# Score tiles of 64x64, masks made on the chip, paged memory and a fixed list of finer steps in a three-part kernel

## The chip, the cores and the metric

The program runs on one core of a Trainium2 chip. A core has five engines that matter here, each with its own in-order queue: PE (matrix products), DVE and POOL (element-wise work), ACT (functions such as exp, sin and gelu, and copies) and SP (which issues the loads and stores). The metric is the device time of one execution in microseconds, the median of several. The time before is 423.65 us (three runs, 423.07 to 424.15).

## The reference

Three parts follow one another, on 2 batches of 768 tokens:

1. Attention with 8 heads of 64. Every query sees the keys less than 16 positions away, and beside them 24 summaries of blocks of 32 keys (the maximum of the keys, the mean of the values). One softmax runs over both:

```
scores_l_m = np.where(mask_l, scale * q @ k^T, -1e9)            # mask_l: |i - j| < 16
scores_s   = scale * q @ k_sum^T + log(32)
a = softmax(concat([scores_l_m, scores_s]))
out = a @ concat([v, v_sum])
```

2. A rotation and a mix over tokens, with d_model 512 (x is the attention's output, all heads side by side):

```
theta = x @ w_theta
y = w_tok_r @ (x * cos(theta)) + w_tok_i @ (x * sin(theta))
u = x + y;   x = u + relu(u @ w_ch)
```

3. A gated block: `h = gelu(x @ w_in)`, split into u and v of 512 columns; v is normalised over its columns and times g_ln; `v_s = w_sg @ v + b_sg` mixes tokens; the output is `x + (u * v_s) @ w_out`.

All of it is float32.

## The kernel before

**Products.** A float32 product is three products: each operand is split into a high part (a rounded copy, L257 to L264) and a low part (the difference, L267), and `mm3` (L269 to L274) adds hi·hi, hi·lo and lo·hi. So L272, L273 and L274 stand for all dense products, in pieces of 512 or 256 columns: theta, the token mix y, ch (u @ w_ch), iv and iu (x @ w_in), sg (w_sg) and o (w_out). A weight comes in by a DMA (L346) and is put together by ACT (L357, `t`) and DVE (L363, `r`), or comes in whole (w_sg, L375); it is copied as its high part by ACT or POOL (`h`) and gets its low part by DVE or POOL (`l`).

**Attention.** It works in 16 units: a unit is a pair of heads and half of a batch's tokens (384 queries). `S` (L485 to L499) makes the scores of both heads in two PSUM banks of 128x360: per head first a product of identity and mask (L485, 128x360), then the near scores in 64x64 tiles of PE (L492, 12 products of 64x96), then the scores against the 24 summaries in tiles of 64x128 (L499, 6 products of 128x24). Then DVE takes the maximum (`m`, L509, both heads in one step) and subtracts it (`d`, L517), ACT does exp (L523), PE transposes (`PT`, L528), ACT or DVE copies (`Pt`), PE multiplies by the values (`O`, L542), DVE divides by the sum (`n`, L552 to L556), PE transposes the result (`X`, L565) and it is copied and split (`xe`, `xh`, `xl`). The key summaries `ks` are made by DVE (L440), the value summaries `vs` by DVE (L448) or POOL (L451, L453); PE turns them (`vp`) and they are spread into the value tiles (`vm`, `vr`). Identity and masks come by one DMA of 244 KB (`cst`, L299), and DVE turns them into bf16 (L301 to L308). Eight products of a tile of zeros (`fill`, L314) open PE's work.

**Rotation.** For each of 12 theta tiles: `kk` and `kb` on ACT, `ra` (L605) and `rr` (L611) on DVE, `ab` (L626, L627), two sines on ACT (`sc`), the product with x (`zm`, L641), high and low part (`zh`, `zl`). y adds up over the 6 token tiles of a batch; it comes in two column halves for each batch, and in each step of six products it needs one z tile and the weights w_r or w_i and w_ri of its token tile. `uv` (L689) adds y to x.

**The order.** No loop sets it. Every step is declared with its engine or engines, what it follows, what memory it takes and a due time (`key`). `Order.play` (L95 to L175) then plays the whole program against a table of costs, takes at each turn the engine that can start first and the most urgent step that it can start, chooses between engines where several may do a step, and so writes down one order. The steps are emitted in that order; every engine runs its own part of it in order. A dense chain (all contraction blocks of ch, iv, iu, sg or o into one bank) is one step, 12 or 18 products long, and so waits for all its operands.

**The memory.** Fixed slots (L206, L207): 27 of 4 KB a partition, 19 of 2 KB, 4 of 6 KB, and small ones; each tile takes a whole slot of its kind, and a load can be issued only when a slot of its kind is free and some are left over (`spare`). [...]

Of the kernel before, what the change touches and what calls it, by code (L numbers as in the profile page):

```python
# [9 lines left out]
F32 = mybir.dt.float32  # L10
# [10 lines left out]
DM = 512  # L21
P = 128
# [14 lines left out]
PI_LO = 3.1415925  # L37

class Op:
# [3 lines left out]
class Order:  # L45

    LAT = {"PE": 0.16, "DVE": 0.09, "ACT": 0.09, "POOL": 0.09, "SP": 0.0}
    RATE = 3.1e-6  # L50
    TABLE = 1.29
    PATIENCE = {"PE": 0.1, "DVE": 0.1, "ACT": 0.1, "POOL": 0.1, "SP": 0.0}

    def __init__(self, slots):
        self.ops, self.by = [], {}
        self.slots, self.kind, self.uses = slots, {}, {}

    def op(self, name, eng, fn, after=(), new=(), use=(), key=None, tab=None, spare=0, size=0,
           port=(), lead=0.0, early=0.0):
        o = Op()  # L60
        o.name, o.eng, o.fn, o.key, o.tab, o.spare = name, eng, fn, key, tab, spare
        o.size, o.port, o.lead, o.early = size, port, lead, early
        o.after, o.new = set(after), list(new)
        o.use = list(use) + [b for b, _ in new]
        o.succ, o.pre, o.left = [], [], len(o.after)
        assert name not in self.by, name
        self.by[name] = o
        self.ops.append(o)
        for b, k in new:
            self.kind[b] = k  # L70
        for b in o.use:
            self.uses[b] = self.uses.get(b, 0) + 1
        return name

    def link(self):

        for o in self.ops:
            for a in o.after:
                self.by[a].succ.append(o)
        left = {o: len(o.succ) for o in self.ops}  # L80
        todo = [o for o in self.ops if not left[o]]
        while todo:
            o = todo.pop()
            d = min(o.eng.values()) + 0.1
            if o.size:
                d = 2.0 + o.size * self.RATE
            k = min((s.key for s in o.succ), default=1e6) - d - o.lead
            o.key = k if o.key is None else o.key
            for a in o.after:
                a = self.by[a]  # L90
                left[a] -= 1
                if not left[a]:
                    todo.append(a)

    def play(self):  # L95
        self.link()
        free_at = {"PE": 1.4, "DVE": 0.7, "ACT": 2.0, "POOL": 0.7, "SP": 0.7}
        slots = {k: [(0.0, s) for s in v] for k, v in self.slots.items()}
        uses, ends, self.where = dict(self.uses), {}, {}
        port = dma = 0.0  # L100
        table = "none"
        waiting = [o for o in self.ops if not o.left]
        out = []

        def able(o, e):
            t = max(free_at[e], o.early)
            for end, on in o.pre:
                t = max(t, end if on == e else end + self.LAT[on])
            return max(t, port) if e in o.port else t

        def room(o):
            t = 0.0
            kinds = [k for _, k in o.new]
            for k in set(kinds):
                c = kinds.count(k) + o.spare
                if len(slots[k]) < c:
                    return None
                t = max(t, sorted(slots[k])[c - 1][0])
            return t

        while waiting:
            found = {}
            for o in waiting:
                t = room(o)
                if t is not None:
                    for e in o.eng:
                        found.setdefault(e, []).append((max(t, able(o, e)), o))
            assert found, [o.name for o in waiting]
            picks = []
            for e, c in found.items():  # L130
                s0 = min(s for s, _ in c) + self.PATIENCE[e]

                def rank(x):
                    o = x[1]
                    turn = 4.0 if e == "ACT" and o.tab and o.tab != table else 0.0
                    return (o.key + turn, x[0])
                s, o = min((x for x in c if x[0] <= s0), key=rank)
                picks.append((s, e, o))
            s, e, o = min(picks, key=lambda x: (x[0], x[1] != "POOL"))
            if len(o.eng) > 1:  # L140

                t = room(o)
                for e2, d in o.eng.items():
                    s2 = max(t, able(o, e2))
                    if (s2 + d < s + o.eng[e] - 0.02
                            and not any(x.key < o.key and q <= s2 + d for q, x in found[e2])):
                        e, s = e2, s2
            if e == "ACT" and o.tab and o.tab != table:
                table = o.tab
                s = max(s, free_at[e]) + self.TABLE  # L150
            waiting.remove(o)
            f = free_at[e] = s + o.eng[e]
            if e in o.port:
                port = f
            if o.size:
                dma = max(dma, s + 1.1) + o.size * self.RATE
                f = dma + 0.9
            o.start, o.end, o.on = s, f, e
            for b, k in o.new:
                j = max((x for x in slots[k] if x[0] <= s + 1e-9), key=lambda x: x[0])  # L160
                slots[k].remove(j)
                self.where[b] = j[1]
            for b in o.use:
                uses[b] -= 1
                ends[b] = max(ends.get(b, 0.0), f + self.LAT[e])
                if not uses[b]:
                    slots[self.kind[b]].append((ends[b], self.where[b]))
            for q in o.succ:
                q.pre.append((f, e))
                q.left -= 1  # L170
                if not q.left:
                    waiting.append(q)
            out.append(o)
        assert len(out) == len(self.ops), [o.name for o in self.ops if o not in out][:20]
        return sorted(out, key=lambda o: o.start)  # L175
# [3 lines left out]
def kernel(  # L179
# [22 lines left out]
    EN = {"PE": nc.tensor, "DVE": nc.vector, "ACT": nc.scalar, "POOL": nc.gpsimd, "SP": nc.sync}  # L202
    PE, DVE, ACT, POOL = nc.tensor, nc.vector, nc.scalar, nc.gpsimd


    SIZE = {"W": 1024, "H": 512, "X": 3 * DM, "K": NS, "V": VC, "Z": 512, "B": 512}  # L206
    COUNT = {"W": 27, "H": 19, "X": 4, "K": 12, "V": 3, "Z": 3, "B": 8}  # L207
    order = Order({k: [f"{k}{j}" for j in range(n)] for k, n in COUNT.items()})
    op = order.op
    made = {}  # L210

    def T(name, dt=F32, fresh=False):

        if name not in made or fresh:
            k = order.kind[name]
            n = SIZE[k] * 4 // mybir.dt.size(dt)
            made[name] = (ps_ if k == "B" else cp).tile([P, n], dt, tag=order.where[name],
                                                        name=name)
        return made[name]


    cst = cp.tile([P, P + 3 * WC], F32, tag="cst", name="cst")
    ident = cst[:, :P]
    identb = cp.tile([P, P], BF16, tag="identb", name="identb")
    maskb = cp.tile([P, 2, 3, WC], BF16, tag="maskb", name="maskb")
# [4 lines left out]

    def act(n):
        return 0.20 + 0.00083 * n

    def dve(n):
        return 0.15 + 0.00105 * n

    def dve1(n):
        return 0.15 + 0.00053 * n

    def pool1(n):  # L240
        return 0.12 + 0.00100 * n

    def pool2(n):
        return 0.12 + 0.00250 * n

    PORT = ("DVE", "POOL")

    def copies(n, es, psum=False):

        d = {"ACT": act(n), "DVE": dve(n) if psum else dve1(n), "POOL": pool1(n)}  # L250
        return {e: d[e] for e in es}

    def diffs(n, es):
        d = {"DVE": dve(n), "POOL": pool2(n)}
        return {e: d[e] for e in es}

    def copy(e, dst, src):  # L257
        if e == "ACT":
            ACT.activation(dst, src, AF.Copy)  # L259
        elif e == "POOL":  # L260
# [14 lines left out]

    def sl(c, n=P):
        return slice(c * n, (c + 1) * n)

    def cut(hl, s):
        return hl[0][:, s], hl[1][:, s]  # L280


    def set_consts(e):
        POOL.memset(half_pi[:], math.pi / 2)
        POOL.memset(eps_t[:], 1e-6)
        for j in range(COUNT["Z"]):
# [712 lines left out]
```

## Time and profile before

| | |
|---|---|
| device time, median of 3 (lowest to highest) | 423.65 us (423.07 to 424.15) |
| span of the profiled execution | 417.5 us |
| what lies around the span (median less span) | 6.15 us |
| PE busy | 397.3 us, 95% |
| DVE busy | 251.6 us, 60% |
| ACT busy | 191.1 us, 46% |
| POOL busy | 111.2 us, 27% |
| loads and stores | 40.71 MB, 98 GB/s over the span |

The span is the time from the first to the last instruction of one profiled execution, and all durations of rows come from that execution. Its own device time is not listed beside it, so the median stands for it. [...] Where the text speaks of a pace, it is the distance between starts in an unbroken row of like instructions.

### The profile page before, as it was taken

The page shows a single profiled execution, that of the slowest core. Times are in us where ns is not written, and L with a number is a line of the kernel's source. Part 1 is how long each engine was busy: PE and PEld are TensorE (multiplying, and loading weights), DVE is VectorE, ACT ScalarE, POOL GpSimd, SP SyncE. Part 2 cuts the span into 40 slices and gives each one's busy share as a digit, 9 for nine tenths or more (in the row PEclk, how much of TensorE's full clock was granted, in tenths as well). Part 3 has the DMA queues.
Part 4 walks back from the last instruction along what each step waited for, and adds up shares of the span by engine and source line. Part 5 has one row for each costly group of instructions (what it writes and reads, how often), then busy time and mean ns, then how long its engine had stood idle before and what let it go on. Part 6 is the DMA issues. An engine that isn't in the chain of part 4 may idle for free.

```text
span 417.5 us, 7283 instructions
## 1 busy us (share of the span) xinstructions
PE 397.3 (95%) x2880; PEld 330.3 (79%) x2880; DVE 251.6 (60%) x459; ACT 191.1 (46%) x332; POOL 111.2 (27%) x147
## 2 busy tenths in 40 slices
PE   7999798989899599999999999999999999999996
PEld 3777576867778388888888898888888989888876
DVE  6589879888966577443564785539574231565222
ACT  2488788876865686224133621435633123421000
POOL 2374663463520523121267521101101000000000
PEclk9699999999999789999999999999999999999999
DMA  8999944341005801200227100100400000210222
GB/s 256 309 325 396 315 155 120 105 124 50 2 2 158 344 2 51 75 2 7 70 83 226 58 2 0 52 0 1 152 0 0 2 0 8 94 52 25 102 75 101
DMA packets 17233, 40.71 MB, mean 98 GB/s; under 512 B 2096, under 2 KB 7600, under 8 KB 17200
## 3 DMA queue, kind: packets, MB, share of 16 engines
q1 hardware_dynamic: 17200, 40.26, 29.6%
q8 instruction: 22, 0.36, 0.4%
q14 instruction: 11, 0.09, 0.1%
HBM read 37.11 MB, written 3.15 MB: 96 GB/s over the span
## 4 chain that ended last, share of the span: by engine, by line
PE 80%; DMA 9%; DVE 6%; issue 1%; ACT 1%; POOL 1%; SPq 0%; DVEq 0%; ACTq 0%
PE y L274 5%; PE y L273 5%; PE y L272 5%; PE sg L274 4%; PE sg L273 4%; PE sg L272 4%; PE ch L272 3%; PE ch L274 3%; PE ch L273 3%; PE iu L274 3%; PE iu L272 3%; PE iu L273 3%; PE iv L274 3%; PE iv L272 3%; PE iv L273 3%; PE ys L274 3%
## 5 line engine op out<-in xcount | busy, mean ns | idle before, releaser
L267 DVE TENSOR_TENSOR z<-f,z 128x512 fp32r<-128x512 f32 x19 | 14.4, 758 | 23.9 <-POOL z L261 20.2
L272 PE MATMUL ys<-w_ri,z 128*128 128x256 f32 x96 | 27.3, 284 | 0.5 <-POOL w_ri L261 0.5
L273 PE MATMUL ys<-w_ri,z 128*128 128x256 f32 x96 | 27.4, 285 | 0.3 <-DVE w_ri L267 0.3
L274 PE MATMUL ys<-w_ri,z 128*128 128x256 f32 x96 | 27.2, 283 | 0.0
L261 POOL TENSOR_SCALAR z<-f 128x512 fp32r<-128x512 f32 x17 | 10.9, 640 | 48.6 <-PE ys L274 27.4
L860 DVE SCALAR_TENSOR_TENSOR gf<-sg,g_sb,bsg 128x512 f32<-128x512 f32 (+1 forms) x16 | 9.9, 616 | 22.5 <-PE sg L274 22.4
L272 PEld LDWEIGHTS ys<-w_ri,z 128*128 128x128 f32 x96 | 18.4, 192 | 5.1 <-POOL w_ri L261 1.0
L272 PE MATMUL y<-w_r,z 128*128 128x512 f32 x48 | 19.9, 415 | 2.7 <-POOL z L261 1.7
L273 PEld LDWEIGHTS ys<-w_ri,z 128*128 128x128 f32 x96 | 18.3, 191 | 5.2 <-DVE w_ri L267 0.8
L272 PE MATMUL th<-w_th,xh 128*128 128x512 f32 x48 | 20.2, 420 | 2.0 <-ACT w_th L259 1.7
L274 PE MATMUL y<-w_r,z 128*128 128x512 f32 x48 | 19.7, 411 | 1.7 <-DVE z L267 1.6
L273 PE MATMUL y<-w_r,z 128*128 128x512 f32 x48 | 19.6, 409 | 0.9 <-POOL w_r L267 0.9
L273 PE MATMUL th<-w_th,xh 128*128 128x512 f32 x48 | 19.0, 395 | 1.0 <-DVE w_th L267 1.0
L509 DVE TENSOR_REDUCE m<-S 128x3 f32<-128x360 f32 x32 | 15.5, 525 | 6.9 <-PE S L499 6.7
L273 PE MATMUL y<-w_i,z 128*128 128x512 f32 x48 | 19.3, 401 | 0.3 <-DVE w_i L267 0.3
L272 PE MATMUL y<-w_i,z 128*128 128x512 f32 x48 | 19.5, 406 | 0.0
L274 PE MATMUL y<-w_i,z 128*128 128x512 f32 x48 | 19.2, 399 | 0.0
L274 PE MATMUL th<-w_th,xh 128*128 128x512 f32 x48 | 18.9, 394 | 0.0
L273 PE MATMUL sg<-w_sg,vn 128*128 128x512 f32 x48 | 18.9, 394 | 0.0
L272 PE MATMUL sg<-w_sg,vn 128*128 128x512 f32 x48 | 18.9, 394 | 0.0
L274 PE MATMUL sg<-w_sg,vn 128*128 128x512 f32 x48 | 18.9, 394 | 0.0
L542 PEld LDWEIGHTS O<-v,Pt 120*64 120x64 f32 x384 | 13.8, 145 | 6.3 <-issue 2.2
(314 smaller groups left out, 1233.5 us busy)
## 6 DMA issues: line engine op xcount, KB each, us to landing
v<-in_vW_dram SPq DMA_DIRECT2D x16, 290.2 KB, 7.9
k<-in_kT_dram SPq DMA_DIRECT2D x8, 384.0 KB, 4.5
q<-in_qT_dram SPq DMA_DIRECT2D x16, 192.0 KB, 6.2
vT<-in_vT_dram SPq DMA_DIRECT2D x8, 384.0 KB, 5.9
w_r<-in_w_rT_dram SPq DMA_DIRECT2D x6, 511.8 KB, 7.3
w_i<-in_w_iT_dram SPq DMA_DIRECT2D x6, 511.8 KB, 6.5
w_th<-in_w_theta_dram SPq DMA_DIRECT2D x4, 511.8 KB, 8.9
w_ch<-in_w_ch_dram SPq DMA_DIRECT2D x4, 511.8 KB, 8.4
```

What stands on the lines that cost most here:

```text
L261: POOL.tensor_scalar(out=dst, in0=src, scalar1=1.0, scalar2=0.0, op0=ALU.mult, op1=ALU.add)
L267: EN[e].tensor_tensor(out=lo, in0=src, in1=hi.bitcast(F32), op=ALU.subtract)
L272: PE.matmul(ps, ah, bh, start=first, stop=False, skip_group_check=True)
L273: PE.matmul(ps, ah, bl, start=False, stop=False, skip_group_check=True)
L274: PE.matmul(ps, al, bh, start=False, stop=last, skip_group_check=True)
L509: DVE.tensor_reduce(out=T(f"m{u}")[:, 3 * h:3 * h + 3], in_=s3(h), axis=AX.X, op=ALU.max)
L542: PE.matmul(ps[64 * ab:64 * ab + 64, o:o + 65], sb[:WC, t * P + 64 * ab:t * P + 64 * ab + 64], v[:WC, c:c + 65], start=True, stop=True)
L860: DVE.scalar_tensor_tensor(out=gf, in0=T(bk)[:, :n], scalar=g_sb[:, f:f + 1], in1=T("bsg")[:, o:o + n], op0=ALU.mult, op1=ALU.add)
```

## The change

- **Scores in 64x64 tiles throughout.** The mask is added by 4 products of 64x(3x96) per unit in place of 2 of 128x360, and the summaries' scores are made by 12 products of 64x24 in place of 6 of 128x24. `m` is two steps, one a head.
- **Masks made by POOL.** DVE fills identity and masks with constants, and 14 `affine_select` instructions on POOL cut them to shape; DVE makes the bf16 identity and one copied mask. The DMA of `cst` is gone, and with it L299 to L308.
- **Memory in pages.** One area of 2760 pieces of 64 bytes in pages of 192 pieces (12 KB); a tile is a piece of any size at an address. A page holds one kind at a time: F (float32) or R (the split float32r form). When a step puts the other kind into it, the page is taken anew under the same tag, so that the first writer follows all users of the page's earlier content.
- **A fixed list.** `Order` with its costs and keys is gone. `PLAN` names every step with its engine and the addresses of what it makes, and `Steps.play` emits them as they stand.
- **Finer steps.** A dense chain has one step for each contraction block (`chain`: three products), so that steps of other chains can stand between them.

Of the list two of its lines are shown; the others are of the same form.

```diff
+AREA, PAGE = 2760, 192
...
+k1.S.2712 ones.V masks.G q0_0.S.2688 q1_0.S.168 warm.V.148 fill.P.0 k0.S.100 ks1.V.0 q2_1.S.76
+identb.V S1_0.P.0.1 ks0.V.1 m1_0_1.V.2 m1_0_0.V.3 q0_1.S.52 S0_1.P.2.3 vT0.S.4 vT1.S.336 k2.S.288
...
+    def play(self, plan):
+        done = set()
+        for step in plan.split():
+            name, e, *at = step.split(".")
+            o = self.all[name]
+            assert all(a in done for a in o.after) and e in o.eng and len(at) == len(o.new), name
+            for (b, kind, n), a in zip(o.new, at):
+                self.where[b] = self.place(kind, n, int(a))
+            o.fn(e)
+            done.add(name)
...
+    def place(kind, n, a):
+        if kind in "FR":
+            j, a = divmod(a, PAGE)
+            if pages.get(j, "-")[0] != kind:
+                w = 16 * min(PAGE, AREA - j * PAGE)
+                pages[j] = kind, cp.tile([P, w], F32 if kind == "F" else F32R, tag=f"page{j}",
+                                         name=f"page{j}{kind}")
+            return pages[j][1][:, 16 * a:16 * a + n // 4]
...
+    def set_masks(e):
+        select(ident, [[-1, P]], 0, 1, 0.0)
+        select(ident, [[1, P]], 0, -1, 0.0)
+        for j, o in ((0, 0), (1, 16), (4, 32)):
+            for r in (0, 64):
+                m = maskb[r:r + 64, j]
+                select(m, [[1, WK]], 15 - o, -1, NEG)
+                select(m, [[-1, WK]], 15 + o, 1, NEG)
...
         def scores(e):
             k, q, ks = T(f"k{p}"), T(f"q{u}"), T(f"ks{p}")
-            s = [T(f"S{u}_{h}") for h in range(2)]
-            for h in range(2):
-                PE.matmul(s[h][:, :3 * WC], identb[:], maskb[:, hf].rearrange("p t c -> p (t c)"),
-                          start=True, stop=False, skip_group_check=True)
+            for ab in range(2):
+                for h in range(2):
+                    rr, m = slice(64 * h, 64 * h + 64), hf + ab
+                    PE.matmul(s3(h)[sl(ab, 64), :, :WK], identb[rr, rr], maskb[rr, m:m + 3],
+                              start=True, stop=False, skip_group_check=True)
...
             for t in range(3):
-                for h in range(2):
-                    rr = slice(64 * h, 64 * h + 64)
-                    PE.matmul(s[h][:, t * WC + WK:(t + 1) * WC], q[rr, sl(t)], ks[rr, :],
-                              start=False, stop=True, skip_group_check=True)
+                for ab in range(2):
+                    for h in range(2):
+                        rr = slice(64 * h, 64 * h + 64)
+                        PE.matmul(s3(h)[sl(ab, 64), t, WK:], q[rr, sl(2 * t + ab, 64)],
+                                  ks[rr, :], start=False, stop=True, skip_group_check=True)
...
+    def chain(bk, n, terms):
+
+        for j, (an, a, bn, b) in enumerate(terms):
+            op(f"{bk}_{j}", "P",
+               lambda e, a=a, b=b, j=j: mm3(T(bk)[:, :n], a(), b(), j == 0, j == len(terms) - 1),
+               after=[an + "l", bn + "l"] + [f"{bk}_{j - 1}"] * (j > 0),
+               use=[an, bn] + [bk] * (j > 0), new=[] if j else [(bk, "B", 1)])
+        return f"{bk}_{len(terms) - 1}"
```

What the list moves is seen in the instructions of each engine. The first place is POOL's start. Before, POOL sets its constants (half_pi, eps, zero, ones) and then makes its first copy, that of the ones into a value tile; the ISA row is the instruction that loads POOL's function library.

```order
L284 MEMSET half_pi 128x1
L285 MEMSET eps_t 128x1
L288 MEMSET zero_72 128x512
L288 MEMSET zero_74 128x512
L288 MEMSET zero_76 128x512
L292 MEMSET ones_78 128x1
L292 MEMSET ones_80 128x1
L292 MEMSET ones_82 128x1
L261 ISA
L261 TENSOR_SCALAR v_1_116<-ones_78 24x774
```

In the changed kernel POOL starts so (ident is the identity, maskb the masks, stage what zero was, page0F the first value tile to be summed):

```order
L360 ISA
L360 AFFINE_SELECT ident<-ident 128x128 x2
L360 AFFINE_SELECT maskb<-maskb 64x96 x12
L384 MEMSET half_pi 128x1
L385 MEMSET eps_t 128x1
L387 MEMSET stage_83 128x512
L387 MEMSET stage_84 128x512
L387 MEMSET stage_85 128x512
L482 TENSOR_TENSOR page0F<-page0F 128x24x16
```

The library's load has moved ahead of all of POOL's work, and between it and the first scores now stand the 14 selects, since every `S` needs masks and the bf16 identity.

The second place is SP, where the last weights of the token mix are loaded (w_r, w_i, w_ri; in_w_rT and in_w_iT are their sources) beside the attention of the second batch (k, q, vT, v). Before, from the 65th of SP's rows:

```order
L430 DMA q_0_1298<-in_qT_dram 128x384
L424 DMA vT_1306<-in_vT_dram 128x768
L435 DMA v_0_1344<-in_vW_dram 96x774
L430 DMA q_1_1418<-in_qT_dram 128x384
L435 DMA v_1_1438<-in_vW_dram 96x774
L346 DMA w_i_1785<-in_w_iT_dram 128x2047
L346 DMA w_r_1839<-in_w_rT_dram 128x2047
L346 DMA w_ri_1843<-in_w_rT_dram 128x1023
L346 DMA w_ri_1843<-in_w_iT_dram 128x1023
L346 DMA w_i_1853<-in_w_iT_dram 128x2047
L346 DMA w_r_1856<-in_w_rT_dram 128x2047
```

In the changed kernel, at the same place of the attention (its last loads of v, k and q):

```order
L467 DMA page8F<-in_vW_dram 96x774 x2
L414 DMA page11F<-in_w_rT_dram 128x2047
L459 DMA page8F<-in_kT_dram 128x768
L467 DMA page12F<-in_vW_dram 96x774
L414 DMA page5F<-in_w_iT_dram 128x2047
L464 DMA page12F<-in_qT_dram 128x384
L414 DMA page5F<-in_w_rT_dram 128x1023
L414 DMA page5F<-in_w_iT_dram 128x1023
L414 DMA page5F<-in_w_iT_dram 128x2047
L414 DMA page12F<-in_w_iT_dram 128x2047
```

The weights stood behind the last load of the attention; now they stand among its last loads.

## Rows read from the trace of the kernel before

**Rows 1.** Windows: stretch, length; busy of PE, PEld, DVE, ACT, POOL; PEclk, DMA, GB/s.
```profile
0.00:40.00 40.00, 36.13 (x540) 26.74 (x542) 29.27 (x69) 22.68 (x39) 16.89 (x36) 0.91 0.98 318
...
0.00:66.50 66.50, 59.65 (x748) 44.52 (x749) 50.67 (x106) 44.42 (x73) 31.07 (x52) 0.95 0.88 285
66.50:135.90 69.40, 64.52 (x645) 51.34 (x643) 56.58 (x108) 50.74 (x82) 27.70 (x33) 1.00 0.26 77
135.90:150.00 14.10, 9.56 (x33) 6.67 (x33) 9.06 (x14) 10.96 (x19) 6.42 (x7) 0.76 0.64 251
150.00:413.90 263.90, 263.53 (x1459) 227.75 (x1457) 134.84 (x232) 85.00 (x161) 45.99 (x56) 1.00 0.15 48
```

**Rows 2.** Timeline of PE, dense: start, us, engine, line, op, out<-in, shapes, count, [idle before <-releaser].
```profile
48.61 0.40 PE L272 MATMUL th<-w_th,xh 128*128 128x512 f32 x1
...
53.93 0.39 PE L274 MATMUL th<-w_th,xh 128*128 128x512 f32 x1
...
408.11 0.28 PE L272 MATMUL o<-gb,w_out 128*128 128x256 f32 x1
...
413.66 0.28 PE L274 MATMUL o<-gb,w_out 128*128 128x256 f32 x1
```

**Rows 3.** Timeline of PE, attention without a wait.
```profile
76.46 0.82 PE L528 MATMUL PT<-cst,P 128*120 128x128 f32 x6
77.11 0.47 PE L485 MATMUL S<-maskb,identb 128*128 128x360 bf16 x2
77.51 0.73 PE L492 MATMUL S<-k,q 64*64 64x96 f32 x24
78.17 0.85 PE L499 MATMUL S<-ks,q 64*128 64x24 f32 x12
78.95 0.92 PE L542 MATMUL O<-v,Pt 120*64 120x65 f32 x24
79.80 0.50 PE L272 MATMUL y<-w_i,z 128*128 128x512 f32 x1
```

**Rows 4.** Timeline of PE, the first product of y.
```profile
66.18 0.50 PE L272 MATMUL y<-w_r,z 128*128 128x512 f32 x1
```

**Rows 5.** Timeline of DVE, attention.
```profile
6.42 0.95 DVE L448 TENSOR_REDUCE vs<-vT 128x24 f32<-128x768 f32 x1 [0.91 <-DMA vT<-in_vT_dram]
7.29 0.96 DVE L509 TENSOR_REDUCE m<-S 128x3 f32<-128x360 f32 x2
...
24.27 0.96 DVE L509 TENSOR_REDUCE m<-S 128x3 f32<-128x360 f32 x2
25.15 0.52 DVE L517 TENSOR_TENSOR P<-S,m 128x360 f32<-128x360 f32 x1
25.59 0.16 DVE L552 TENSOR_SCALAR ri<-O 128x6 f32<-128x6 f32 x1
...
26.48 0.52 DVE L517 TENSOR_TENSOR P<-S,m 128x360 f32<-128x360 f32 x1
```

**Rows 6.** Timeline of POOL, its first copy.
```profile
9.43 0.84 POOL L261 TENSOR_SCALAR v<-ones 24x774 f32<-24x774 f32 x1 [7.08 <-ACT ones L259]
```

**Rows 7.** One line on POOL: op, tiles, count, ns min/median/max, first and last start.
```profile
L261 POOL TENSOR_SCALAR xh<-xT x3: 513/514/515, 37.6 to 85.8; 128x384 fp32r<-128x384 f32 x3
```

**Rows 8.** Timeline of SP, the late weight, and of PE behind it.
```profile
124.70 0.33 SPq L346 DMA_DIRECT2D w_i<-in_w_iT_dram  x1
...
142.65 0.79 PE L272 MATMUL y<-w_r,z 128*128 128x512 f32 x1 [1.72 <-POOL z L261]
```

**Rows 9.** Timeline of POOL and DVE, two operands from SBUF on each.
```profile
42.70 2.13 POOL L267 TENSOR_TENSOR xh<-xT,xh 128x384 fp32r<-128x384 f32 x2
...
43.89 1.48 DVE L363 SCALAR_TENSOR_TENSOR w_th1r<-w_th,zero 128x512 int32<-128x512 int32 x1
45.30 0.68 DVE L363 SCALAR_TENSOR_TENSOR w_th2r<-w_th,zero 128x512 int32<-128x512 int32 x1
45.90 0.68 DVE L363 SCALAR_TENSOR_TENSOR w_th3r<-w_th,zero 128x512 int32<-128x512 int32 x1
```

More of the change, by code (lines that the diff above doesn't have):

```diff
@@ L37 @@
 PI_LO = 3.1415925
-class Op:
-    pass
[L45 to L72, printed above, removed]
-        return name
[L75 to L175, printed above, removed]
@@ L209 @@
[L209 to L223, printed above, removed]
+    banks = [ps_.tile([P, 512], F32, tag=f"B{j}", name=f"bank{j}") for j in range(8)]
@@ L308 @@
-    op("masks", {"DVE": 1.4}, set_masks, after=["cst"])
-    def filler(n):
-        def f(e):
-            ps, warm = T("warmb"), T("warm")
-            for j in range(n):
-                PE.matmul(ps[:], warm[:, :P], warm[:, P:640], start=True, stop=True)
-        return f
-    op("fill", {"PE": 3.4}, filler(8), after=["warm0"], use=["warm"], new=[("warmb", "B")], key=-100)
-    units = {}
-    def high_low(key, src, after, new, spare=0):
-        nm = "w_%s%d" % key
-        def high(e):
-            t = T(nm, F32R, fresh=True)
-            units[key] = (t[:, :512], t[:, 512:])
-            copy(e, t[:, :512], src())
-        op(nm + "h", copies(512, ("ACT", "POOL")), high, after=[after], port=("POOL",),
-           use=[nm + "r"] + ([] if new else [nm]), new=new, spare=spare)
-        op(nm + "l", diffs(512, ("DVE", "POOL")),
-           lambda e: diff(e, units[key][1], src(), units[key][0]), after=[nm + "h"], port=PORT,
-           use=[nm + "r", nm])
@@ L691, in mixed @@
+                op(f"uv{b}_{d}_{half}", "V", ev, after=pre + [f"xl{b * NP + d}_{x}" for x in hf],
                    use=[f"y{b}_{d}" if half == 0 else f"ys{b}_{h}"])
[L693 to L707 removed]
@@ L709, in hl @@
-    def hl(kind, b, d, half):
-        n = HALVES[half][1]
-        t = T(f"{kind}{'ab'[half]}{b}_{d}")
-        return t[:, :n], t[:, n:2 * n]
+    for p in range(B * NP):
+        at_pair(p)
+    for n in range(B * NT):
+        theta(n)
+        for h in range(2):
+            rotated(n, h)
+    for b in range(B):
+        for h in range(2):
+            mixed(b, h)
+    for c in range(4):
+        unit("ch", c, [rows(w_ch, c)])
+        unit("inv", c, [rows(w_in, c)[:, 512:]])
+        unit("inu", c, [rows(w_in, c)[:, :512]])
+        unit("out", c, [rows(w_out, c)])
@@ L798, in in_v @@
-            op(f"vo{b}_{i}", {"DVE": 0.54}, norm, after=[f"rv{b}"], use=[f"vf{b}_{i}"], port=("DVE",))
-            ub = [f"vn{b}_{i}"] if b else sorted({f"vn{b}_{x // 3}" for x in (2 * i, 2 * i + 1)})
-            vb[b, i] = ub
-            new = [(x, "W" if b else "X") for x in ub if x not in bufs]
-            bufs |= set(ub)
-            op(f"vh{b}_{i}", copies(512, ("ACT", "POOL")),
-               lambda e, i=i: copy(e, vn(i)[0], T(f"vf{b}_{i}")[:]), after=[f"vo{b}_{i}"],
-               use=[f"vf{b}_{i}"] + [x for x in ub if x not in [y for y, _ in new]], new=new,
-               port=("POOL",))
@@ L940, in _layout @@
+    steps.play(PLAN)
 def _layout(inputs):
```

868 lines of the change are left out of this document (465 added, 403 removed).

## The prediction

> **What bounds the kernel now.** I read the busy times first, then windows by stage, then PE's timeline for the pace of each kind of work, and last DVE, POOL and SP where PE waits. PE is busy 95% of the span, so the first question is how much of that is work. An unbroken row of 512-column products advances 0.2313 us a product (23 steps from 48.61 to 53.93), one of 256 columns 0.1181 (47 steps from 408.11 to 413.66) [rows 2]. The dense work has 1008 products of 512 columns and 720 of 256: 233.2 + 85.0 = 318.2 us. One unit of attention costs PE 1.84 for S (77.11 to 78.95), 0.65 for PT, 0.85 for O [rows 3]; its three X transposes cost half a PT, 0.33. Times 16 that is 29.4 + 10.4 + 13.6 + 5.2, and some 0.9 for the eight `vp`: 59.5. Together PE has 377.7 us of work, and its last product ends at 413.66 + 0.28 = 413.9 [rows 2]. So 36.2 us of PE's time are lost, and a change of order can win no more than that.
>
> Where are they lost? Between 150 and 413.9 PE is busy 263.53 of 263.90 [rows 1]: nothing. Ahead of the first product of y (66.2 [rows 4]) the order has 10 S, 18 halves of PT and of O, 8 X, 5 `vp` and 20 theta steps of three products: 18.4 + 5.9 + 7.7 + 2.6 + 0.5 + 13.9 = 49.0, so 17.2 are lost there (the eight fill products among them). From 135.9 to 150 PE has 33 products, half of them narrow: 33 x 0.175 = 5.8 of 14.1, 8.3 lost; the granted clock is 0.76 there, after gaps of PE, so part of its 9.56 busy us are slow products [rows 1]. The remaining 10.3 lie between 66.2 and 135.9.
>
> What holds PE ahead of the first y? The DMA engines are busy 0.98 of the first 40 us at 318 GB/s [rows 1], and DVE passes every unit. By pace DVE takes 0.87 for a `ks` or `vs`, 0.44 for each half of m or d, 0.89 for an n [rows 5], 0.60 for a two-operand instruction of 512 columns [rows 9]. Its order ahead of the first y: 8 x 0.87, 18 halves of m and 18 d, 9 n, 8 copies and splits of 384 columns (at d's 0.44), 17 of the 0.60 kind, small ones 2.4 (estimated): 46.9. So 19.3 of 66.2 are waits and slow-downs: 4.1 before the first m at 7.29 [rows 5] (3.2 of work stand ahead of it), 15.2 behind it. After 135.9 it is the weights: the last w_i is issued only at 124.70, behind all loads of attention, and PE still waits for a z at 142.65 [rows 8].
>
> **The change, part by part.**
>
> *S in 64x64 tiles.* The mask now costs 0.40 for two products of 360 columns, the summaries 0.78 for 12 passes, the near scores 0.66 for 24 passes in 64x64 tiles [rows 3]. Four mask products of 288 columns in quarter tiles: if two run side by side and all columns count, 0.40 x (288/360) / 2 = 0.16; if none does, 0.64. I take 0.20, since the near scores advance by 0.03 a pass, which single file would not give. The summaries' 24 passes of 24 columns: 0.33 if half the price of a pass of the same kind, 0.66 at its price, 0.78 if nothing is won. I take 0.66, the same tile. S becomes 1.52: -0.32 x 16 = -5.1; with all ends 1.15 to 2.08, -11 to +3.8. PE's work: 372.6.
>
> *Masks on POOL.* Before, the library load (the ISA row) lies behind the constants and in the idle 7.08 before POOL's first copy at 9.43, whose end is put to ACT [rows 6]: it costs nothing, and takes between 0 and 7.1. Now it stands ahead of the selects, and every S waits for those. A select has no row; a copy of 384 columns takes 0.51 [rows 7] and one of 774 columns 0.84 [rows 6], so I put 96 to 128 columns at 0.27: 14 x 0.27 = 3.7 (2 to 7 as ends). With the whole 7.1 from 0.7 on, the selects end at 11.5, the bf16 identity at 11.9, the first S and m come at 13.4; with a load of no length at about 7, where they are now. I take the long end, for nothing in the row excludes it. [...] PE idles from the fill products to this first S, and its first units may run at a lower clock, as it did after the gaps at 135.9 to 150; DVE and the loads set the pace there, so I count it at nothing, and at most at 2.
>
> *The first stage.* DVE's order ahead of the first y now has 9 long reductions, 19 halves of m, 18 d, 9 n, 12 copies and splits, 15 of the 0.60 kind, small ones 1.8: 48.2. Ahead of the first m stand 2.9 of it, so the late start costs 10.5. Of the 15.2 behind it I keep a third, 5: six units are scored before anything else, so DVE has some 10 us of m and d in hand while the loads run. First y at 48.2 + 10.5 + 5 = 64 (with ends of 0 and 15.2 for the waits, 59 to 74). The loads agree: 18.2 MB are issued before the first y's step in the old list, 17.5 in the new (no `cst`, a k and a v less, a q more), 0.7 MB / 318 GB/s = 2.2 us sooner than 66.2. PE's work there is 15.2 + 5.9 + 7.7 + 2.6 + 0.6 + 21 x 0.694 = 46.6, so 17.4 are lost: as much as before. POOL, which takes over high and low parts of weights, has some 38 us there, beside DVE: where both read two operands, one DVE instruction went from 0.68 to 1.48 [rows 9]. That is in the 5.
>
> *The middle.* The 10.3 between 66.2 and 135.9: DVE and ACT have less to do for the second batch's attention (POOL takes it), and y of the first batch's second half stands between. I halve them, 5.2; ends 0 and 10.3.
>
> *The late weights.* They are now among the last attention loads, and the DMA engines are at 0.26 there [rows 1]. I keep 2 of 8.3; ends 0 and 8.3.
>
> *The dense end.* Finer chain steps change no work, and nothing is lost there now: 0, or +2 if the list holds PE somewhere. Behind the last product 417.5 - 413.9 = 3.6 stay: one addition and one store as now.
>
> Sum: 372.6 + 17.4 + 5.2 + 2 + 0.4 = 397.6; + 3.6 = 401.2 span. The median lies 6.15 above the profiled span: **407**.
>
> **The rivals.**
>
> *The library load costs nothing here* (the near end of [rows 6]), or the loads hide it. The first m comes at 7 and DVE could bring the first y to 58, but 17.5 MB at 318 GB/s and 2 us of start allow about 58 to 60 [rows 1]: -4; with a middle of half the loss, -2.6: 400. For it: before, the idle is put to ACT, not to POOL. Against: that row says nothing of the length.
>
> [...] Each engine's list is in order; the 15.2 on DVE stay whole, as [rows 9] shows for POOL beside DVE and as POOL now has half as much work again: first y at 74, +10: 417. For it: DMA at 0.98 is no matter of order. Against: DVE has six units in hand early.
>
> *Slower: pages that change their kind.* A page taken for the other kind lets its first writer wait for every user of 12 KB, not of its own piece; the writer (a high part on POOL or ACT, or a load on SP) stands at the head of its queue, and whoever is behind waits with it, PE at the end. By the list a page changes kind about 17 times, 4 of them ahead of the first y (w_th0's high part the first, on POOL, with x's splits behind it). If each costs PE what the wait at 142.65 cost, 1.72 [rows 8], that is 29: 436, or some 430 where a few hide. It decides from 16.4 / 17 = 0.96 a change on, or as soon as the first y comes later than 81. Against: three quarters of the changes lie where PE has 150 us of queued chains.
>
> *The masks are not what they say*: if S gets no cheaper (+3.8 instead of -5.1) it is 416, within the second rival's range.
>
> **How the numbers follow.** 407 has 0.48 (its own range 402 to 413), 400 has 0.20 (396 to 402), 417 has 0.17 (413 to 422), 430 has 0.15. The range of 8 in 10 is 398 to 420. Within 0.3% of 423.65 (1.3 us, what a measurement can tell) lies 0.04, from the upper edge of 417 and the lower of 430; slower 0.15; faster 0.81.
>
> **What would show it.** The first AFFINE_SELECT at about 7.8, the last before 12, and the first m near 13.4 (right) or 7 (first rival). S from mask to last summary 1.5, its mask row 0.2. First y at 62 to 66; at 74 the second rival holds, past 81 the last. No stretch of PE between 120 and 150 with a clock under 0.9; w_i and w_r issued before 115. A PE that stays at 0.2313 a product from 150 to the end. I am wrong if PE's loss past the first y is above 15, or if a high part's row shows an idle of several us put to other tiles of its page.

## The result and the profile after

The changed kernel takes 400.4 us (median of 4 runs, 398.91 to 401.41) against 423.36 for the kernel before, run beside it: a ratio of 0.944 with a 95% interval of 0.939 to 0.949. Ratios, and medians of the kernel before from here on, leave out slow runs, those more than 1.5% above the fastest of the same kernel. The forecast was 407 in a range of 398 to 420. Its profiled execution has a span of 398.6 us. That execution took 400.38, so only 1.8 us lie around the span. The medians differ by 23.0 us and the two profiled spans by 18.9: the profiled execution of before was a fast one, so the comparison by stages below accounts for 18.9 us, and in which stage the other 4.1 lie is not shown.

First the stages of the changed kernel. The columns are those of [rows 1].

```profile
0.00:41.00 41.00, 31.86 (x615) 25.88 (x616) 27.48 (x61) 18.06 (x31) 21.64 (x51) 0.79 0.98 315
...
66.00:130.00 64.00, 61.35 (x738) 51.57 (x738) 58.40 (x106) 55.21 (x100) 36.33 (x35) 0.97 0.43 137
130.00:395.10 265.10, 265.10 (x1477) 231.31 (x1476) 134.00 (x214) 67.80 (x130) 118.55 (x116) 1.00 0.13 45
```

From 130 us to the end PE is never idle. The stretch of [rows 1] with a clock of 0.76 is gone. POOL has taken over much of the dense part's work (118.6 us behind 130).

Next PE's timeline, one unit's S, the first product of y and the last product, which answer to [rows 2 to 4].

```profile
73.74 0.32 PE L516 MATMUL bank<-maskb,identb 64*64 64x288 bf16 x4
73.89 0.66 PE L523 MATMUL bank<-page13F,page11F 64*64 64x96 f32 x24
74.38 0.48 PE L530 MATMUL bank<-small,page11F 64*64 64x24 f32 x24
74.79 0.57 PE L568 MATMUL bank<-page12F,page7F 120*64 120x65 f32 x12
```

```profile
66.07 0.41 PE L337 MATMUL bank<-page10R,page2R 128*128 128x512 f32 x1
...
395.10 0.28 PE L339 MATMUL bank<-page3R,page13R 128*128 128x256 f32 x1
```

S takes 1.05 us (73.74 to 74.79) where it took 1.84: mask 0.15, near scores 0.49, summaries 0.41. PE's work is now 318.2 + 16 x 1.05 = 16.8 for S + 30.1 for the rest of the attention = 365.1. Its last product ends at 395.4, so 30.3 us are lost. The first y starts at 66.1, as before. The work ahead of it is 49.0 before, and now 46.6 - 10 x 0.47 = 41.9. So the losses compare as follows:

| PE's time lost, us | before | forecast | after |
|---|---|---|---|
| ahead of the first y | 17.2 | 17.4 | 24.2 |
| behind it | 19.0 | 7.6 | 6.1 |
| PE's work | 377.7 | 372.6 | 365.1 |

In these two executions the end of the last product moved by 18.5 us, and all of it lies behind the first y: 5.5 less work (six S at 0.79, one theta step that the new list does earlier) and 12.9 fewer lost. Ahead of the first y, ten cheaper S gave nothing in this pair; the executions differ there from one to the next, and "What sets the first y" below compares more of them.

Last, what PE waited for: releaser, sum, times, longest ("issue" is a wait for nothing that the view knows). These are the six longest of the whole execution.

```profile
PE bank L530 <- issue: 3.3, 1, 3.3
PE bank L590 <- DVE page7F L581: 2.4, 1, 2.4
PE bank L393 <- DVE page0F L352: 1.7, 1, 1.7
PE bank L516 <- DVE page1F L541: 1.6, 1, 1.6
PE bank L523 <- DMA page0F<-in_qT_dram: 1.0, 1, 1.0
PE bank L523 <- issue: 0.9, 1, 0.9
```

These are all the waits of 0.9 us or more; none of them is for a z or a weight, as the one at 142.65 was [rows 8].

### The profile page after: what moved, and what is told of

Its sections match the earlier page's. It is cut to its first block, busy times and chain, and to the rows that moved or that the text cites. A ratio compares the mean times of both kernels' runs of the same rounds, so it can differ in the third digit from the quotient of the medians.

```text
span 398.6 us, 7716 instructions
## 1 busy us (share of the span) xinstructions
PE 382.7 (96%) x3104; PEld 328.3 (82%) x3104; DVE 243.2 (61%) x426; ACT 161.2 (40%) x291; POOL 194.6 (49%) x219
## 4 chain that ended last, share of the span: by engine, by line
PE 81%; DVE 5%; issue 1%; DVEq 0%
PE bank L337 26%; PE bank L338 25%; PE bank L339 25%; PE bank L568 2%; PE bank L554 1%; PE bank L523 1%; DVE small L535 1%; PE bank L590 1%; DVE xT L329 0%; PE bank L530 0%; DVE small L472 0%; DVE page1F L644 0%; DVE page8F L541 0%; PE bank L516 0%; DVE page5F L541 0%
## 5 line engine op out<-in xcount | busy, mean ns | idle before, releaser
L815 DVE SCALAR_TENSOR_TENSOR page5F<-bank,g_sb,page8F 128x256 f32<-128x256 f32 (+1 forms) x11 | 6.6, 602 | 21.4 <-PE bank L339 18.0
L833 DVE TENSOR_TENSOR page5F<-bank,xT 128x512 f32<-128x512 f32 (+1 forms) x15 | 8.1, 564 | 18.2 <-PE bank L339 18.2
L693 DVE TENSOR_TENSOR xT<-bank,xT 128x256 f32<-128x256 f32 (+1 forms) x16 | 8.4, 549 | 17.5 <-PE bank L339 17.5
L535 DVE TENSOR_REDUCE small<-bank 128x3 f32<-128x360 f32 x32 | 16.0, 523 | 4.6 <-PE bank L530 4.6
L754 DVE SCALAR_TENSOR_TENSOR xT<-bank,xT 128x512 f32<-128x512 f32 (+1 forms) x16 | 8.3, 550 | 12.0 <-PE bank L339 12.0
L420 ACT ACTIVATE stage<-page8F 128x512 f16<-128x512 bf16 x8 | 6.1, 785 | 17.8 <-DVE page5F L427 16.8
L820 POOL TENSOR_TENSOR page5F<-page5F,page7F 128x512 f32<-128x512 f32 (+1 forms) x6 | 6.7, 1117 | 12.1 <-ACT page7F L799 12.1
L332 POOL TENSOR_TENSOR page6R<-page1F,page6R 128x512 fp32r<-128x512 f32 x2 | 2.6, 1285 | 17.9 <-DVE page6R L329 16.2
L337 PE MATMUL bank<-page10R,page2R 128*128 128x512 f32 x20 | 8.1, 405 | 0.0
L420 ACT ACTIVATE stage<-page5F 128x512 f16<-128x512 bf16 x8 | 6.3, 792 | 4.2 <-DVE page5F L427 2.6
L338 PE MATMUL bank<-page3R,page2R 128*128 128x256 f32 (+1 forms) x26 | 8.0, 308 | 0.0
L339 PE MATMUL bank<-page3R,page2R 128*128 128x256 f32 (+1 forms) x26 | 8.0, 307 | 0.0
L337 PE MATMUL bank<-page3R,page2R 128*128 128x256 f32 (+1 forms) x26 | 7.9, 305 | 0.0
L338 PE MATMUL bank<-page10R,page2R 128*128 128x512 f32 x20 | 7.9, 395 | 0.0
L339 PE MATMUL bank<-page10R,page2R 128*128 128x512 f32 x20 | 7.8, 391 | 0.0
L338 PE MATMUL bank<-page4R,page6R 128*128 128x256 f32 (+1 forms) x24 | 7.7, 320 | 0.0
```

Source lines behind the costliest of these rows:

```text
L337: PE.matmul(ps, ah, bh, start=first, stop=False, skip_group_check=True)
L338: PE.matmul(ps, ah, bl, start=False, stop=False, skip_group_check=True)
L339: PE.matmul(ps, al, bh, start=False, stop=last, skip_group_check=True)
L420: ACT.activation(T(nm + "s", F16).rearrange("p (n t) -> p n t", t=2)[:, :, 1], raw[:, :, 2], AF.Copy)
L535: op(f"m{u}_{h}", "V", lambda e, h=h: DVE.tensor_reduce(out=T(f"m{u}_{h}"), in_=s3(h), axis=AX.X, op=ALU.max), after=[f"S{u}"], new=[(f"m{ ...
L693: DVE.tensor_tensor(out=dst, in0=ps, in1=dst, op=ALU.add)
```

## Experiments

The kernels were run in three groups, each on one chip with the kernel before beside them, and each ratio is to the kernel before of its own group. Its medians were 421.4, 421.2 and 422.6 in the three groups. The changed kernel, run again in the second group, had 400.17 (ratio 0.952, 0.948 to 0.956); its profiled execution there has a span of 395.8.

> The changed kernel as it is, beside the others on the same chip: both theories 400.4, 1 us either way.

### What the tiles of 64x64 are worth

In the old order, with old memory and the old masks:

```diff
-                PE.matmul(s[h][:, :3 * WC], identb[:], maskb[:, hf].rearrange("p t c -> p (t c)"),
+                    PE.matmul(s3(h)[sl(ab, 64), :, :WK], identb[rr, rr], maskb[rr, m:m + 3],
...
-                    PE.matmul(s[h][:, t * WC + WK:(t + 1) * WC], q[rr, sl(t)], ks[rr, :],
+                        PE.matmul(s3(h)[sl(ab, 64), t, WK:], q[rr, sl(2 * t + ab, 64)], ks[rr, :],
```

> The kernel before with one part of the change: S in 64x64 tiles throughout (4 mask products of 64x288, 12 of 64x24); its own order, its memory, masks still from the DMA. Theory A (S costs 1.05 instead of 1.84 us, since PE no longer changes its tile shape inside S, but the stage ahead of the first y is set by the loads, so that only the six units behind the first y give anything): 6 x 0.79 = 4.7 us less, about 418.5, first y still at 66. Rival B (each of the 16 units gives its 0.79): 12.6 less, about 411, first y near 58. Rival C (the late weights take it all back): 423.

Measured: 416.73, ratio 0.989 (0.985 to 0.994). S is 1.06 there, and the first y starts at 67.9, no sooner than before:

```profile
66.84 0.32 PE L487 MATMUL S<-maskb,identb 64*64 64x288 bf16 x4
66.99 0.67 PE L494 MATMUL S<-k,q 64*64 64x96 f32 x24
67.48 0.48 PE L502 MATMUL S<-ks,q 64*64 64x24 f32 x24
67.90 0.50 PE L272 MATMUL y<-w_r,z 128*128 128x512 f32 x1
```

Theory A holds and B falls: 16 x 0.79 = 12.6 us of PE's work are gone, 0.0107 x 421.4 = 4.5 us of time (2.6 to 6.4) came of it. The late weights kept their stretch (10.25 us busy of 135.9 to 150, clock 0.76).

Then one piece of S at a time back in the changed kernel, first the summaries:

```diff
-                for ab in range(2):
-                    for h in range(2):
-                        PE.matmul(s3(h)[sl(ab, 64), t, WK:], q[rr, sl(2 * t + ab, 64)],
+                for h in range(2):
+                    PE.matmul(s3(h)[:, t, WK:], q[rr, sl(t)], ks[rr, :],
```

> The changed kernel with only the summaries' scores back in tiles of 64x128 (6 products of 128x24). Theory A: the summaries' row goes from 0.41 back to 0.78 and the near scores ahead of it from 0.49 to 0.66, because the switch of tile shape is waited for there; S 1.6; time +0.55 x 6 = 3.3, about 403.7. Rival B (all 16 units count): +8.8, about 409. Rival C (the near scores' price comes from the mask ahead of them): near scores stay at 0.49.

and then the mask:

```diff
-            for ab in range(2):
-                for h in range(2):
-                    PE.matmul(s3(h)[sl(ab, 64), :, :WK], identb[rr, rr], maskb[rr, m:m + 3],
+            for h in range(2):
+                PE.matmul(s3(h)[:, :, :WK], identb[:], maskb[:, hf:hf + 3],
```

> The changed kernel with only the mask back in one product of 128x288 a head (its two row halves hold the two masks; 8 selects on the masks in place of 12, two small DVE copies more). Theory A: the mask's row goes from 0.15 to about 0.33 and a switch of tile shape follows it; S 1.2 to 1.4; time +1 to 2, about 402. Rival C (the near scores become dear behind a wide mask): near scores 0.66 and S 1.5, time +3.

Measured: 402.03, ratio 0.960 (0.950 to 0.970), and 401.01, ratio 0.957 (0.947 to 0.968). The intervals overlap with that of the changed kernel in the second group (0.948 to 0.956), and no run of the changed kernel stands beside them in their own, so of the times only this can be said: each piece is worth a few us at most. The rows tell more. Summaries wide, then mask wide:

```profile
75.70 0.32 PE L516 MATMUL bank<-maskb,identb 64*64 64x288 bf16 x4
75.85 0.67 PE L523 MATMUL bank<-page13F,page11F 64*64 64x96 f32 x24
76.45 0.85 PE L529 MATMUL bank<-small,page11F 64*128 64x24 f32 x12
77.23 0.57 PE L567 MATMUL bank<-page12F,page7F 120*64 120x65 f32 x12
```

```profile
72.37 0.41 PE L515 MATMUL bank<-maskb,identb 128*128 128x288 bf16 x2
72.71 0.73 PE L522 MATMUL bank<-page13F,page11F 64*64 64x96 f32 x24
73.26 0.49 PE L529 MATMUL bank<-small,page11F 64*64 64x24 f32 x24
73.68 0.57 PE L567 MATMUL bank<-page12F,page7F 120*64 120x65 f32 x12
```

| start to start, us | mask | near scores | summaries | S |
|---|---|---|---|---|
| before [rows 3] | 0.40 | 0.66 | 0.78 | 1.84 |
| only the summaries wide | 0.15 | 0.60 | 0.78 | 1.53 |
| only the mask wide | 0.34 | 0.55 | 0.42 | 1.31 |
| after | 0.15 | 0.49 | 0.41 | 1.05 |

The 24 passes of the near scores are the same instructions in all four kernels. Where the granted clock is 1.00 they take 0.49 when their neighbours have their tile shape, 0.06 more behind a wide mask, 0.11 more ahead of wide summaries, and 0.17 more with both. Each side carries a part, so the 0.66 expected of one neighbour alone came from neither. The rows agree with a price of 0.06 to 0.11 for each change of the tile shape; what makes it, they do not show. The larger part of the gain is the narrow pieces themselves: the mask 0.40 to 0.15, the summaries 0.78 to 0.41.

### What sets the first y

Fewer loads with the same instructions (only half of each q and v tile is loaded, and read twice):

```diff
-                T(f"q{p}_{hf}"), qT[b, r, :, 384 * hf:384 * hf + 384]),
+                T(f"q{p}_{hf}")[:, :192], qT[b, r, :, 384 * hf:384 * hf + 192]),
-                T(f"v{p}_{hf}")[:WK], vW[b, r, :, VH * hf:VH * hf + VH]),
+                T(f"v{p}_{hf}")[:WK, :VH // 2], vW[b, r, :, VH * hf:VH * hf + VH // 2]),
```

> The changed kernel with only half of each q and v tile loaded; the other half's instructions read the loaded half again, so every instruction stays and only the loads shrink (13 x 96 KB + 11 x 145 KB = 2.85 MB less of 17.5 ahead of the first y). Theory A (the loads set the first stage, 308 GB/s): first y up to 9 us sooner than 66, at 57 to 60, and the time 6 to 9 less, about 392. Rival B (DVE or the fixed list sets it): first y at 64 or later, time 398 to 400.

Measured: 396.48, ratio 0.941 (0.937 to 0.946), 3.7 us below the changed kernel beside it. Its first y starts at 61.7, 3.1 us sooner than in the changed kernel's second execution (64.8). Theory A gave 6 to 9, rival B nothing; it lies between, for the time as well. The windows of this kernel show what takes over:

```profile
0.00:41.00 41.00, 33.38 (x659) 26.77 (x660) 30.02 (x69) 20.99 (x37) 23.61 (x54) 0.88 0.97 317
41.00:66.00 25.00, 24.10 (x257) 19.77 (x256) 24.12 (x45) 20.41 (x34) 20.78 (x20) 1.00 0.53 151
```

Behind 41 us DVE and PE are each busy 24.1 of 25, with the DMA engines half idle. So the loads have a share in the first 40 us, and DVE with PE hold the next 25; taking bytes away moves only the first part. The changed kernel itself agrees: from 41.05 to its first y at 66.07 PE has, by pace, 23.1 us of work (an estimate), so some 22 of the 24.2 lost lie ahead of 41.

Kernels whose list ahead of the first y is the same show by chance how the DMA rate goes with it. The rate of the first 41 us differed from execution to execution: 318 GB/s went with a first y at 63.5 (the kernel without POOL's share, below), 305 with 64.8 (changed kernel, second execution), 285 with 66.5 (whole chains, below); the clock was 0.92 in all three. Two others come later than these would have it, the changed kernel's first execution (315 GB/s, 66.1) and the first try with whole chains (304, 66.2); their clocks of 0.79 and 0.83 may be why. The first of the three:

```profile
0.00:41.00 41.00, 30.93 (x631) 24.08 (x632) 29.49 (x66) 19.72 (x34) 22.46 (x52) 0.92 0.98 318
```

```profile
63.49 0.41 PE L352 MATMUL bank<-page10R,page2R 128*128 128x512 f32 x1
```

The execution of before also had 318 GB/s, and a clock of 0.91 [rows 1], and its first y came at 66.2. So at a like rate and clock the new list is 2.7 us sooner (one execution each), which the pair of executions above hides. The tiles alone do not show it: by the three executions 10 GB/s are worth some 0.9 us (an estimate from three points), and the kernel with tiles alone (301 GB/s, first y at 67.9) is about as much later than before as its lower rate gives.

There is a second wait in this stage. PE's stops put to "issue" fall at a count of products, not at a step. Ahead of the longest one PE has done 473 products in the changed kernel, in the kernel without POOL's share and in the one with a wide mask, whose S have fewer products, so that another step stands there:

```profile
0.00:28.87 28.87, 23.04 (x473) 18.03 (x474) 20.77 (x46) 11.86 (x22) 16.82 (x46) 0.88 0.95 301
```

```profile
0.00:28.04 28.04, 21.57 (x473) 16.21 (x474) 20.60 (x46) 12.16 (x22) 16.55 (x46) 0.94 0.95 304
```

```profile
0.00:30.89 30.89, 24.01 (x473) 17.08 (x474) 22.28 (x51) 12.98 (x23) 16.75 (x43) 1.00 0.97 286
```

The others come behind 222, 347 to 349 and 599 or 600 products, 125 to 127 apart. The DMA view has a queue of its own for instructions, with 24 packets in the changed kernel for PE's 3104 products, 129 each:

```profile
q8 instruction: 24, 0.39, 0.4%
```

In the traces of the twelve runs other than before PE goes on 2.4 to 3.0 us behind the start of one of these packets of 16 KB, at all 32 such stops (in the changed kernel at 14.37 behind a packet of 11.89, and at 32.18 behind one of 29.41). By this timing PE stood there for its own instructions, while the DMA engines were busy 0.95 to 0.97 in the three windows above; no experiment moved them. These stops sum to 4.2 us ahead of the first y in the changed kernel and to none in the kernel before; narrow tiles make more and shorter products of an S (52 in place of 38), so that PE is through with a packet sooner. How much of the gain of ten S they took was not tried.

The low clock leads to the next one, products that nobody reads in PE's early waits:

```diff
+WARM = {"0_1": 4, "0_0": 4, "2_0": 6, "2_1": 4, "1_1": 4, "3_0": 8}
...
+            for j in range(WARM.get(u, 0)):
+                PE.matmul(banks[7][:, :480], identb[:], maskb[:].rearrange("p t c -> p (t c)")[:, :480],
+                          start=True, stop=True) if u != "3_0" else PE.matmul(
+                    T(f"S{u}_0")[:, :480], identb[:],
+                    maskb[:].rearrange("p t c -> p (t c)")[:, :480], start=True, stop=True)
```

> The changed kernel, and a version meant to be faster: ahead of six S units of the first stage (0_0, 0_1, 1_1, 2_0, 2_1, 3_0) stand 4 to 8 products of identity and masks that nobody reads, so that PE is busy where it waits and its clock doesn't fall (0.61 to 0.87 in 28 to 41 us of two executions). Theory A (the lower clock costs part of the first stage): clock 0.95 or more up to 41 us, first y 1 to 2 us sooner than 65 to 66, time 398 to 399. Rival B (loads and DVE set the pace, the clock doesn't matter): no difference, 400. Rival C (the 30 products stand in PE's queue ahead of real work): +2 to +4.

Measured: 401.79, ratio 0.952 (0.948 to 0.956), that of the changed kernel in the second group. Beside it in its own group stands the kernel with masks by DMA (399.59, below), 2.2 us less, so rival C's +2 isn't excluded. The clock did stay at 0.96 up to 41 us, but this execution had 277 GB/s and its first y came at 68.2. It isn't faster; what the clock alone costs in this stage stays open.

A version meant to be faster, whose vT of the first batch is not loaded at all (PE adds up the values):

```diff
+                PE.matmul(T(f"vp{p}")[:NS, :VC],
+                          sel[:WK, (64 * w - FIRST[w]) // 16, NS - 2 - 2 * w:2 * NS - 2 - 2 * w],
+                          T(f"v{p}_{hf}")[:WK, i * VC:(i + 1) * VC], start=w == 0, stop=w == NW - 1)
```

> The changed kernel, and a version meant to be faster with the same output: for the first batch's four head pairs vT is not loaded and not summed by POOL and DVE; PE adds up the value blocks from the v tiles by 12 products of 24x129 with a matrix of ones and zeros (6 selects and 2 memsets more at the start). Theory A (loads set the first stage): 4 x 384 KB = 1.57 MB less, at 308 GB/s first y 5 us sooner, 395 to 396. Rival B (the list waits elsewhere, or the products and the wait for both v tiles cost PE what the loads give): 400 or more.

Measured: 405.35, ratio 0.963 (0.960 to 0.967): slower than the changed kernel by 5.2. Rival B. On PE the products of a pair are two groups of 12 passes of some 1.34 us (8 groups, 10.7 us), and what stands behind them in PE's queue waits. DVE's timeline shows it:

```profile
31.51 0.16 DVE L601 TENSOR_SCALAR small<-bank 128x6 f32<-128x6 f32 x1 [5.45 <-ACT page0F L326]
...
37.40 0.28 DVE L331 COPY sums<-bank 24x129 f32<-24x129 f32 x1 [4.91 <-PE bank L498]
```

Its first y came at 71.5. An in-order queue with 24 us of lost time is no place for 11 us of extra work when that work stands ahead of what DVE waits for.

### The masks

```diff
+    op("ones", "S", lambda e: nc.sync.dma_start(xT[:, 0, :P + 3 * WC], consts))
...
+    op("masks", "V", set_masks, after=["ones"])
```

> The changed kernel with identity and masks loaded by one DMA of 244 KB at the head of SP's queue again, and 7 DVE copies in place of the 14 selects. Theory A (the library load costs nothing and the selects end when the first loads land; POOL's first sums come 1 to 2 us sooner, the loads 0.8 us later): within 1.5 us of 400. Rival B (the selects hold the first S): first S before 5.3, and 2 or more less.

Measured: 399.59, ratio 0.947 (0.943 to 0.951), between the changed kernel's 0.944 and 0.952, so no difference is seen. With the DMA the first S starts at 7.14, with POOL's selects at 5.30, and the first y at 66.1 in both. Where the masks come from makes no difference here.

### The blocks of the dense chains

A first try put all 76 chains in one piece, at the place of their last block. There, 11 of them read memory that the list has already given to other data, so the kernel computes something else and its 410.66 says nothing of the chains.

> The changed kernel with each dense chain (ch, iv, iu, sg, o) in one piece again: all its blocks stand where the list has its last block; nothing else is moved. Theory A (from 150 us on PE lost nothing before the change either, so single blocks between other chains buy nothing): 400 to 402. Rival B (the blocks fill waits that whole chains would show, with the new list's timing of the operands): +4 to +10, and PE idle between 130 and 330.

The second leaves those 11 in blocks:

```diff
-    steps.play(PLAN)
+    steps.play(whole(PLAN))
...
+        if dense and bank not in AS_BEFORE:
+            held.setdefault(bank, []).append(step)
+            if int(j) < (5 if name[:2] == "sg" else 3):
+                continue
+            rest += held[bank]
```

> The changed kernel with 65 of its 76 dense chains in one piece (all blocks stand where the list has the last one); the other 11 stay in blocks, since their operands' memory is taken anew before the last block. Theory A (PE lost nothing from 150 on before the change, so blocks buy nothing): 400 to 402. Rival B (with the new list's timing of weights and splits the blocks fill waits): +4 to +10, with PE idle between 130 and 330.

Measured: 416.85, ratio 0.991 (0.987 to 0.994), 16.7 us above the changed kernel. Rival B, and more. The stretch from 200 to 330 us, where the changed kernel is never idle, and PE's two longest waits there and behind it:

```profile
200.00:330.00 130.00, 122.76 (x642) 105.22 (x641) 68.89 (x111) 32.26 (x54) 54.09 (x54) 0.97 0.05 16
```

```profile
218.24 0.58 PE L357 MATMUL bank<-page9R,page0R 128*128 128x256 f32 x1 [5.14 <-DVE xT L713]
...
338.72 0.39 PE L357 MATMUL bank<-page2R,page6R 128*128 128x256 f32 x1 [2.79 <-DVE page7F L835]
```

The new list brings operands of the dense part just in time, block by block (uv, and ga, the scaled and shifted result of sg, are late here), and a whole chain waits for its last one. A list made anew for whole chains was not tried, so 16.7 us is what the blocks are worth in this list, not in any.

### POOL's share

```diff
-    steps.play(PLAN)
+    steps.play(off_pool(PLAN))
...
+        if on and e == "G" and "V" in ENGINES(name):
+            step = ".".join([name, "V", *at])
```

> The changed kernel with the 37 low parts and products with x (zl, zm, xl, weights' and u's l) that the list gives to POOL between the first y and the first ch back on DVE, in the same places of the list. Theory A (DVE is busy 58 of 64 us there, and 37 x 0.60 = 22 us more can't pass): first ch 8 to 15 us later, time 408 to 415. Rival B (POOL's two-operand work slows DVE as much as it relieves it): 400 or less.

Measured: 405.64, ratio 0.963 (0.958 to 0.968), 6 us above the 399.59 of the kernel with masks by DMA beside it: less than expected, in theory A's direction. The window that answers to the changed kernel's second row:

```profile
66.00:130.00 64.00, 57.43 (x707) 46.89 (x707) 59.65 (x117) 50.28 (x89) 10.81 (x15) 0.97 0.43 134
```

DVE takes over 37 instructions and is hardly busier (59.7 of 64 against 58.4), since it was nearly full already; PE is busy 3.9 us less there.

## Why the prediction was right, and where its steps were not

**Faster, and in the range: right.** Of the rivals the first one, with its 400, came out in time and in its premise, the library load without a cost (no idle of POOL is put to it, and the first select starts at 1.14). That its time fits is luck: its 4 us were to come from a first y at 58 to 60, and the first y came at 63.5 to 66.5. The way was partly another than either sum.

**S: the term was mis-sized.** Forecast -0.32 a unit, measured -0.79, which is outside the bounds I gave (-11 for 16 units, measured -12.6). The near scores were taken as unchanged (0.66), but 0.17 of that belonged to the tile shapes beside them; and the summaries' passes were priced like near scores (0.66) and took 0.41. The mask's 0.20 was close (0.15).

**The library load: wrong end taken.** I put 7.1 us on it and the first m at 13.4. The first select ran at 1.14 and its 0.63 of idle is put to DVE's constants; the first m came at 8.0:

```profile
1.14 0.66 POOL L360 TENSOR_SCALAR_AFFINE_SELECT ident<-ident 128x128 f32<-128x128 f32 x2 [0.63 <-DVE ident L355]
1.75 3.96 POOL L360 TENSOR_SCALAR_AFFINE_SELECT maskb<-maskb 64x96 bf16<-64x96 bf16 x12
```

```profile
8.01 0.96 DVE L535 TENSOR_REDUCE small<-bank 128x3 f32<-128x360 f32 x2
```

The last wait ahead of the first m is for a load (DVE stood 1.90 for a key tile), not for the selects. And the idle of [rows 6] was a wait for ACT, as the row said; ACT wrote those ones just ahead of POOL's start at 9.43:

```profile
8.99 0.27 ACT L259 ACTIVATE ones<-vp 24x128 f32<-24x128 f32 x1 [6.97 <-PE vp L457]
```

How long the load itself takes, no run shows.

**The first y: right number, wrong make-up.** Forecast 64, measured 63.5 to 66.5 in executions of the same list. (The sum by bytes counts in units of 1024: its 18.2 and 17.5 are 18.6 and 17.9 MB. Their difference stays 0.7.) The sum had 10.5 us of late start and 5 of gaps on DVE; in the profile the late start is 8.0 - 2.9 = 5.1 and the gaps 66.1 - 48.2 - 5.1 = 12.8. That the two errors cancel in the sum is luck. The other estimate, by bytes (2.2 us sooner than 66.2), gave the same 64; at a like DMA rate the new list is 2.7 sooner, but the experiment with half loads gave 3.1 us for 2.85 MB, a third of what 308 GB/s would give, so bytes alone do not set it. The cheaper S of ten units were swallowed: PE lost 24.2 where 17.4 were forecast, 4.2 of it in the stops for instructions, which the sum put at nothing.

**Behind the first y: right.** 7.6 lost were forecast and 6.1 measured; the late weights are gone as a wait. All but one of them are issued by 114.3, against 124.7 to 134.3 before, and the last w_r at 124.3, not ahead of 115. Moving these loads alone was not tried. The sign of a clock of 0.9 or more between 120 and 150 held: 1.00 from 120 on. Moving POOL's two-operand work back to DVE costs 6 us, so "POOL takes it" is borne out.

**The dense end: right as a difference, for an incomplete reason.** I wrote that blocks change nothing because nothing was lost there. Nothing is lost now either, but in this list the blocks carry 16.7 us: they are the cover under which operands may come late. That this is what freed the engines ahead of 130 us is likely; it was not tried by itself.

**What lies around the span: mis-sized.** 6.15 was the median less one span. The runs of the changed kernel that list both show 1.8 (400.38 and 398.6), so the profiled execution of before was one of the faster ones. The span itself was forecast at 401.2 and measured 398.6: S -7.5, ahead of the first y +6.8, behind it -1.5, the tail -0.4. These four and the 4.35 around the span make up the 6.9 by which 407.3 was too high.

**Pages that change their kind: no sign of it.** None of PE's long waits is put to such a writer. The first such writer, w_th0's high part on POOL at 27.47, shows 3.26 of idle, put to a weight's load; its source was ready at 26.96, so at most 0.5 of it can be the page's. A list without changes of kind was not tried.

## What to carry to other kernels

Price a step by its neighbours too: the near scores between two other tile shapes took 0.66 us in place of 0.49, and a row's start to start contains that. Work taken off an engine is worth what it moves at the wait that ends last; ten of sixteen cheaper units lay in a stage whose DMA engines were busy 0.98 of the first 41 us, and gave nothing that could be seen. And a part of a change that looks free in the old order can be what the new order stands on, so it has to be undone in the new one to be judged.

## What the runs showed of the hardware that was not expected

- The same 24 passes of 64x96 took 0.49 to 0.66 us by the tile shapes ahead of and behind them.
- The same list ahead of the first y took 63.5 to 66.5 us in five executions, with DMA rates of 318 to 285 GB/s and clocks of 0.79 to 0.92 in the first 41 us.
- PE stood 3.3 us in the middle of a unit's S at 28.9 us, with the DMA engines at 0.98 in that stage; 2.8 in the kernel without POOL's share. Such stops came some 126 products apart, and PE went on 2.4 to 3.0 us behind the start of a 16 KB packet of the instruction queue.
